# A gated convolution in sixteen array parts, plain v loaded in pieces, and a new fixed order

## The chip, the cores and the metric

The kernel runs on one core of a Trainium2 chip. The metric is the device time of one execution in microseconds (us). A core has five engines that run side by side, each with its own instruction stream: TensorE (PE; its weight loads are listed as PEld), VectorE (DVE), ScalarE (ACT), GpSimd (POOL) and SyncE (SP), which here only issues DMA transfers.

## The reference

Two layers stand one behind the other. The first is attention over 8 batches, 8 heads, 576 positions and 64 columns a head. Heads 0 to 3 look back over a plain window of 32 positions, heads 4 to 7 over every fourth of the last 128.

```python
scores = scale * np.matmul(q, k.transpose(0, 1, 3, 2))
mask_plain = (rel >= 0) & (rel < window)                                    # window 32
mask_dil = (rel >= 0) & (rel < window * dilation) & (rel % dilation == 0)   # dilation 4
attn = np.exp(scores - max); attn = attn / (attn.sum(-1) + 1e-9)            # masked scores are -1e9
x = np.matmul(attn, v)            # then heads side by side: (8, 576, 512)
```

The second is a gated linear unit with a causal convolution of five taps, each of the 512 channels for itself:

```python
for k in range(5):
    gate_pre += conv_w[k][None, None, :] * xp[:, k:k + S, :]                # xp: x with 4 zeros ahead
out = (1 / (1 + np.exp(-gate_pre)) * (x @ w_val)) @ w_out
```

Inputs and outputs are float32; the kernel computes in bfloat16 with float32 accumulation.

## The kernel before, in words

All work is cut into 733 tasks, each the instructions of one engine for one step. `plan.add(name, engines, function, deps, tens)` makes a task, and `ORDER` at the top of the file writes out in which order they are emitted and on which engine: `177P` is task 177 on TensorE, the letters being P, A, V, G, S for PE, ACT, DVE, POOL, SP, and a number behind the letter is a count of warm-up matmuls (L659) ahead of it. `HOMES` says which buffer of its class (`COUNTS`) each tensor takes. Every engine works through its own part of that order from first to last, so a task that waits holds up all tasks of its engine that stand behind it.

Per batch there is a plain half and a dilated half, and each consists of two units of two heads:

- SP loads q, k and v. Plain v (`load_vp`, tile `vp`) comes in runs of 64 floats: 18 runs a partition for the first four batches (`NAT`), 24 for the others, as one DMA. Dilated v (`vd`) is one DMA of longer runs. Loads marked `big` form a chain: each waits until the fifth big one before it has landed (`DEPTH`).
- POOL or ACT casts dilated v to bfloat16 (`vn`, task U), and for the first four batches moves rows of plain v to other partitions (`vw`, tasks HA to HD, `SHIFTS`).
- PE transposes q and k (L464 dilated, L401 plain), ACT or DVE copies them out (`qT`, `kT`).
- PE computes scores of three query blocks (L333, task S, 6 matmuls), ACT takes the exponential (L340), DVE multiplies with a mask (L347). PE multiplies with v (L356, task A, 12 matmuls; v has a column of ones for the sum), DVE takes the reciprocal (L365) and scales (L366, task N).
- PE transposes the result (L428 plain, 6; L488 dilated, 16), and a copy puts it into `xT`, channels on partitions.

Two batches form a group. `gated` cuts the 1152 positions of a group into three blocks of 384 columns, the last group into four of 288. For each block and each half `cp` of the channels (two chunks of 128) there are four tasks. The convolution (C) multiplies `xT`, shifted by the tap, with a diagonal matrix of weights, `conv_diag`, in 64x64 array parts: 5 taps x 2 chunks x 2 row halves are 20 matmuls (L530), and the four that stand together use the four different quarters of the array. ACT takes tanh (L540, task G; sigmoid is 0.5 + 0.5 tanh of half the argument), PE computes the values (L548, task V, 8 matmuls), and DVE multiplies (L558, task Y). One row half of every second chunk lands in the other half of the partitions; the rows and columns of w_val and w_out are permuted to fit when POOL casts them (tasks Wv and Wo), in 24 and 7 copies. Every value task waits for all of w_val, every output task for all of w_out.

`outputs` makes 36 tiles of 128 positions: 4 matmuls (L577, task O), an eviction on ACT (L584) or DVE (L586), a store by SP (L590).

PSUM, where PE writes, is cut into three two-bank buffers (`pd`, class `ps2`: scores, attention times v, plain transposes, convolution, values) and two one-bank buffers (`pu`, class `ps1`: dilated transposes, outputs). A convolution half takes one `pd`, its value task another.

Of the kernel before, what the change touches and what calls it, by code (L numbers as in the profile page):

```python
# [16 lines left out]
0G 15S 16S 1S 13S 33P6 14S 34A 48S 17S 47S 49S 2P 31P1 32A 3V 18G 38P2 57P 51G 21P 59V 22V 53G 58V 52G 39A 40V  # L17
19P 35P 20A 26P2 36A 23P 80S 27A 37V 24A 28V 25V 41P2 54P 56A 4S 55A 42V 29P 30V 70P 81S 6G 45P3 5G 43P 50A
60P 73P 7S 46V 71A 44A 74A 8G 112S 61A 96P 84P 63P 64A 149P 72V 97A 75V 76P 98P 85V 65V 62V 82S 66P 77V 86P
67V 150A 99A 100P 78P 87A 101A 83G 103P 88P 89A 79V 68P 69V 104A 113S 105V 119P 114S 120A 91P 92A 145P 151P  # L20
93V 102V 90V 121A 94P 169S 146A 152V 106P 95V 147P 122P 107V 108P 170S 110P 123V 124A 138P 109A 201S 139A 148V
135P 185P 136A 125P 128P 129A 126A 111V 165P 166A 140V 130V 137V 116G 127V 186V 234S 202S 157P 158A 187P 115G
118G 117G 141P 171S 175P 176A 188V 192P 193A 131P 142V 132V 173P 172G 174A 189P 190A 208P 209V 210A 143P 133P
177P 178A 180P 203S 134V 211P 235S 250P 144V 159P 181A 213A 212A 227P 228A 153P 154A 11S 238P 205G 251V 194V
179V 191V 160V 182V 239A 206A 195P 229V 196V 207A 167P 168V 204G 12G 183P 184V 155P 252P 224P 225A 214P 240P
215A 9S 253V 156V 199P 254P 241V 255A 226V 217P 218A 161P 230P 197P 162A 200A 324S 267S 236S 216V 219V 245P
256V 220P 198A 246A 231V 10G 625P 628P 221V 323S 266S 325S 237G 626A 257P 242P 243A 276P 629A 222P 326G 223A
258A 278A 277V 163P 341P 232P 303P 247V 244V 259V 233V 342V 304A 299P 300A 164V 339P 260P 248P 329P 305P 330A
340V 268S 261V 631P 630S 355S 384S 533S 627S 346P 356S 249V 343P 264P 306V 265V 273P 632A 347A 344A 348V 274V
275A 272A 345V 262P 301P 302V 279P 280A 292P 634P 635V 263A 349P 350V 327P 293A 328A 289P 281V 282P 283A 290A  # L30
284V 271G 270G 269G 643P 644A 637P 285P 291V 294V 400P 401V 286V 638A 334P 331P 335A 332A 336V 640P 641A 295P
388P 389A 358P 296V 360A 311P 312A 361P 363A 333V 359V 287P 362V 288V 297P 337P 298A 338V 385S 417S 374P 375A
319P 386S 320A 307P 308A 353P 351P 639S 377P 364P 354V 376V 313P 357S 469S 642S 416S 352A 378A 379V 365A 402P
321P 390P 314V 403V 407P 367P 322V 649P 366V 368A 391A 380P 309P 485P 408A 650A 381V 369V 310V 404P 392P 393A
405A 486V 646P 370P 647A 422P 419P 394V 371V 424V 423A 421A 645S 470S 651S 633S 502S 418S 655P 382P 438P 409V
395P 420A 439A 387G 396A 315P 316A 449P 656A 383V 406V 410P 652P 411V 450A 435P 531S 425P 372P 653A 436A 426A
440V 397V 373V 317P 658P 654S 530S 532S 471S 451P 487P 501S 318V 427V 437V 659A 473P 441P 488A 452V 398P 475P
442V 445P 399V 476A 447P 446A 474A 492P 493A 428P 661P 429A 448V 494V 430V 548P 549V 472G 489P 480P 507P 662A
490A 491V 536P 537V 481A 508A 443P 444V 660S 663S 565S 657S 564S 509A 431P 432V 482V 550P 551A 477P 478A 412P
504P 555P 413A 556A 479V 433P 434V 505A 506A 495P 496V 414P 453P 454A 415V 552P 483P 484V 553A 538P 664P 539A  # L40
523P 510P 511A 524A 520P 521A 676P 570P 665V 497P 567P 677A 569A 568A 554V 557V 571A 636S 461P 462A 522V 525V
572A 534S 667P 463P 503S 498A 666S 648S 455P 535G 670P 671A 526P 464V 668V 456V 527V 566S 673P 558P 682P 559V
674A 672S 669S 678S 583P 586P 587A 584A 499P 588V 683V 500V 457P 458A 465P 466A 513P 585V 459P 460V 528P 589P
529A 514A 590V 679P 680A 691P 573P 540P 541A 576P 574A 577A 685P 515V 512V 692V 686A 516P 681S 684S 687S 517V
467P 591P 518P 605P 468V 519A 597P 606A 601P 578V 575V 592V 543P 602A 688P 579P 542V 544A 598A 580V 599P 689A
545V 603P 581P 582A 600V 546P 694P 547V 604V 695A 697P 698V 609P 593P 560P 562P 561V 563A 610A 594A 595P 675S
696S 690S 699S 703P 700P 704V 596V 701V 607P 608V 706P 709P 611P 612V 705S 702S 693S 621P 617P 710V 613P 622A
711S 707A 708S 715P 712P 716A 618A 713A 614A 615P 616V 714S 619P 623P 721P 722A 718P 719A 620V 624V 727P 717S
723S 720S 724P 728A 725A 729S 726S 730P 731A 732S
"""  # L50

HOMES = "01010210000113130211000021002000132000231120022230241102145110103141020101013010110671123222114010302002121011010121100020122020000113021121100010231011014002232122312230001402035111113121011000001040001271122022114211200220201210102211110120022006000113012301031011031312015002120122131011400020471110130403021302202101000612230101122001201213021121220010101202202400001311141011120300130017102102012110131140321053111213132000031220020210061030221022401013242000210112021202210011202120011203140201100102021003120310041312140112140011020113140211031200110403"
# [11 lines left out]
 'gate': 3,  # L64
# [38 lines left out]
class Plan:  # L103
# [28 lines left out]
    def run(self):  # L132
# [24 lines left out]
def kernel(  # L157
# [28 lines left out]
    GW = 384  # L186
    DA = D + 1
# [31 lines left out]
    ident2 = consts.tile([128, D], BF16, name="ident2")  # L219
# [3 lines left out]
    conv_diag = consts.tile([128, NCH, K, D], BF16, name="conv_diag")  # L223
# [6 lines left out]
    def early():  # L230
# [26 lines left out]
        nc.vector.tensor_copy(ident2[0:64, :], ident[0:64, 0:64])  # L257
        nc.vector.tensor_copy(ident2[64:128, :], ident[64:128, 64:128])
# [35 lines left out]
    def load_vp(b, ten):  # L294
        nat = b < NAT

        def issue():
            if nat:
                o, a = vp[ten.idx][:, 0:18, 0:D], [[D, 128], [128 * D, 18], [1, D]]
            else:  # L300
                o, a = vp[ten.idx][:, :, 0:D], [[D, 128], [QB * D, 4 * NB], [1, D]]
            return nc.sync.dma_start(out=o, in_=src_ap(v, (b * H * S - (0 if nat else W)) * D, a))
        return [load(f"Lvp{b}", ten, issue)]

    SHIFTS = (("HA", ((1, 0, 64, 64, 0), (1, 64, 64, 0, 1)), 1.0),
# [196 lines left out]
    def gated(g, xb, w_ready):  # L502
# [3 lines left out]
        for k in range(n_blk):  # L506
# [13 lines left out]

            for cp in range(2):
                pc, gt, pv = Ten("ps2"), Ten("gate"), Ten("ps2")

                def conv(eng, cp=cp, pc=pc, c0=c0, mov=mov, dst=dst, wd=wd):
                    for kk in range(K):
                        for n in range(2):
                            for hb in range(2):
                                ob = hb if n == 0 else 1 - hb
                                rb = slice(64 * hb, 64 * hb + 64)
                                nc.tensor.matmul(  # L530
                                    out=dst(ps2[pc.idx][64 * ob:64 * ob + 64, n, 0:wd]),
                                    lhsT=conv_diag[rb, 2 * cp + n, kk, :],
                                    rhs=mov(2 * cp + n, rb, c0 + kk - (K - 1)),
                                    start=(kk == 0), stop=(kk == K - 1))
                t_c = plan.add(f"C{g}{k}{cp}", (PE,), conv,
                               deps=[x_done[(b, 2 * cp + n)] for b in last for n in range(2)] + [w_ready["conv"]],
                               tens=[pc, gt, xb], out=pc)
# [58 lines left out]
    def weights():  # L596
# [14 lines left out]
        def conv_e(eng):  # L611
            for to, n, c, frm, ch in ((0, 64, 0, 0, 0), (64, 64, 0, 0, 1), (0, 64, 1, 64, 0), (64, 64, 1, 64, 1), (0, 128, 2, 0, 2)):
# [5 lines left out]
                in0=ident2[:, None, :].to_broadcast([128, NCH * K, D]),  # L618
# [90 lines left out]
```

## Time and profile before

| | us |
|---|---|
| median of 3 runs (lowest, highest) | 173.76 (173.53, 174.15) |
| the profiled execution | 173.37 |
| its span, from the first to the last instruction | 171.7 |
| busy: PE, PEld, DVE, ACT, POOL | 153.0, 102.2, 121.7, 108.4, 44.2 |
| convolution matmuls (L530), 520 | 23.1 busy |
| value matmuls (L548), 208 | 34.9 busy |
| output matmuls (L577), 127 recorded | 33.4 busy |

The profile is one execution. Its page gives busy time by engine, the span in 40 slices (a digit is the busy share in tenths), the DMA queues, the chain of waits that ended last, the costliest groups of instructions, and the DMA issues. Group rows read: line, engine, operation, written tile <- read tiles, shapes, count | busy us, mean ns of one | idle time ahead of them and what ended it. In a table by windows each engine has its busy us and, in brackets, its instructions; then come the granted PE clock, the DMA share and GB/s. SPq is SP issuing. Matmuls are pipelined, so their single durations overlap, and some records of them can be missing.

### The profile page before, as it was taken

Reading aid. Unit: us, or ns where it says so; the run is one execution under the profiler, and the core shown is the slowest. Engines: PE = TensorE matmul, PEld = TensorE weight load, DVE = VectorE, ACT = ScalarE, POOL = GpSimd, SP = SyncE. Lnnn points to the kernel's source line nnn. Section 1 sums busy time; section 2 is a strip of 40 time slices with the busy share of each in tenths; the row PEclk is TensorE's granted clock in tenths of the full one; section 3 lists DMA queues with packets and bytes.
Section 4 is the critical chain, followed back from the end, with each engine's and each line's share of the span. In section 5 each row is a group of like instructions: output and inputs, shape, how many; then the busy total and the mean of one; then the engine's idle time right before and its main releaser. Section 6 shows DMA issues by size and latency. Waiting matters only on the chain.

```text
span 171.7 us, 5752 instructions
## 1 busy us (share of the span) xinstructions
PE 153.0 (89%) x2441; PEld 102.2 (60%) x2460; DVE 121.7 (71%) x243; ACT 108.4 (63%) x182; POOL 44.2 (26%) x82
## 2 busy tenths in 40 slices
PE   6697967888989979899999799989999999999990
PEld 1355654677557546567766567576656577666640
DVE  6549778989899579779788658899368776664220
ACT  2147976198868744798847693888946675242542
POOL 7023998560659427403000000210110000000000
PEclk9999999999999999999999999999999999999999
DMA  4999999999799999999994948969979060333445
GB/s 137 325 355 290 375 370 210 311 374 319 200 383 364 362 269 281 373 353 222 282 328 139 267 115 286 373 165 390 270 202 303 2 244 4 116 119 138 186 165 199
DMA packets 49123, 43.63 MB, mean 254 GB/s; under 512 B 22981, under 2 KB 39365, under 8 KB 49098
## 3 DMA queue, kind: packets, MB, share of 16 engines
q1 hardware_dynamic: 49098, 43.27, 82.2%
q8 instruction: 19, 0.31, 0.7%
q14 instruction: 6, 0.05, 0.1%
HBM read 33.83 MB, written 9.44 MB: 252 GB/s over the span
## 4 chain that ended last, share of the span: by engine, by line
PE 58%; DMA 12%; DVE 11%; ACT 6%; SPq 5%; issue 3%; POOL 3%; ACTq 0%; DVEq 0%; POOLq 0%
PE pu L577 17%; PE pd L548 14%; PE pd L530 9%; DMA qk<-in_k_dram 5%; PE pd L356 5%; DVE et L347 4%; DMA wt<-in_moe_w_out_dram 4%; SPq L281 4%; PE pd L333 4%; DMA qk<-in_q_dram 3%; PE pu L464 3%; POOL w_out L316 3%; PE pd L401 2%; PE pu L488 2%; ACT et L340 2%
## 5 line engine op out<-in xcount | busy, mean ns | idle before, releaser
L340 ACT ACTIVATE et<-pd 128x576 bf16<-128x576 f32 x64 | 39.3, 657 | 10.4 <-PE pd L333 9.3
L347 DVE TENSOR_TENSOR et<-et,mask 128x576 bf16<-128x576 bf16 x64 | 33.9, 557 | 4.7 <-ACT et L340 4.5
L548 PE MATMUL pd<-xT,w_val 128*128 128x384 bf16 (+1 forms) x208 | 34.9, 313 | 0.7 <-DVE xn L366 0.4
L577 PE MATMUL pu<-w_out,yT 128*128 128x512 bf16 x127 | 33.4, 379 | 1.4 <-issue 0.6
L558 DVE SCALAR_TENSOR_TENSOR yT<-gate,pd 128x768 bf16<-128x768 bf16 (+1 forms) x26 | 23.0, 886 | 12.5 <-PE pd L548 8.5
L366 DVE TENSOR_TENSOR xn<-pd,rec 96x768 bf16<-96x768 f32 x32 | 30.5, 954 | 1.1
L316 POOL CAST vn<-vd 128x1536 bf16<-128x1536 f32 x8 | 12.3, 1540 | 70.3 <-DMA vd<-in_v_dram 70.3
L540 ACT ACTIVATE gate<-pd 128x768 bf16<-128x768 f32 (+1 forms) x26 | 19.9, 769 | 10.9 <-DVE yT L558 5.5
L548 PEld LDWEIGHTS <-w_val 128*128 128x128 bf16 x208 | 19.4, 97 | 11.6 <-issue 1.5
L530 PE MATMUL pd<-xT,conv_diag 64*64 64x384 bf16 (+1 forms) x520 | 23.1, 313 | 1.8 <-DVE xT L314 1.1
L584 ACT ACTIVATE osb<-pu 128x512 f32<-128x512 f32 x27 | 16.2, 601 | 11.0 <-PE pu L577 10.7
L577 PEld LDWEIGHTS <-yT 128*128 128x128 bf16 x144 | 12.6, 97 | 13.3 <-issue 1.1
L333 PE MATMUL pd<-qT,kT 64*128 64x96 bf16 x384 | 16.1, 209 | 3.1 <-ACT qT L312 0.9
L530 PEld LDWEIGHTS <-conv_diag 64*64 64x64 bf16 x520 | 15.1, 106 | 6.2 <-issue 2.5
L316 POOL CAST vw<-vp 32x384 bf16<-32x384 f32 (+2 forms) x31 | 16.8, 541 | 7.5 <-DMA vp<-in_v_dram 6.1
L356 PEld LDWEIGHTS <-et 128*128 128x128 bf16 x384 | 14.7, 97 | 6.5 <-DVE et L347 2.5
L464 PE MATMUL pu<-ident,qk 128*128 128x128 bf16 x160 | 14.8, 230 | 3.0 <-DMA qk<-in_k_dram 2.0
L333 PEld LDWEIGHTS <-kT 64*128 64x128 bf16 x384 | 10.1, 96 | 11.5 <-issue 6.3
L464 PEld LDWEIGHTS <-qk 128*128 128x128 bf16 x160 | 10.8, 102 | 7.3 <-DMA qk<-in_k_dram 3.0
L314 DVE COPY xT<-pu 128x576 bf16<-128x576 bf16 x18 | 10.1, 568 | 4.0 <-PE pu L488 3.1
L312 ACT COPY xT<-pu 128x576 bf16<-128x576 bf16 x14 | 8.9, 646 | 6.2 <-PE pu L428 3.6
L365 DVE RECIPROCAL rec<-pd 96x12 f32<-96x12 f32 x32 | 7.1, 223 | 7.6 <-PE pd L356 4.5
(52 smaller groups left out, 146.2 us busy)
## 6 DMA issues: line engine op xcount, KB each, us to landing
out_dram<-osb SPq DMA_DIRECT2D x36, 256.0 KB, 2.7
vd<-in_v_dram SPq DMA_DIRECT2D x8, 768.0 KB, 9.3
qk<-in_k_dram SPq DMA_DIRECT2D x8, 576.0 KB, 7.8
qk<-in_q_dram SPq DMA_DIRECT2D x8, 576.0 KB, 8.0
qk<-in_q_dram SPq DMA_DIRECT2D x6, 640.0 KB, 9.1
qk<-in_k_dram SPq DMA_DIRECT2D x6, 640.0 KB, 8.7
vp<-in_v_dram SPq DMA_DIRECT2D x4, 768.0 KB, 7.9
vp<-in_v_dram SPq DMA_DIRECT2D x4, 576.0 KB, 9.8
```

What stands on the lines that cost most here:

```text
L316: nc.gpsimd.tensor_copy(out_, in_)
L333: nc.tensor.matmul(out=ps2[ps.idx][:, l, QB * jj:QB * jj + QB], lhsT=kT[kt.idx][rb, c:c + 128], rhs=qT[qt.idx][rb, c:c + QB], start=True, ...
L340: nc.scalar.activation(out=et[e.idx][:, 0:2 * HW].rearrange("p (l n) -> p l n", l=2), in_=ps2[ps.idx][:, :, 0:HW], func=AF.Exp, scale=scale)
L347: (nc.vector if eng == DVE else nc.gpsimd).tensor_tensor(out=ev, in0=ev, in1=m, op=ALU.mult)
L356: nc.tensor.matmul(out=ps2[po.idx][:, hf, (2 * jj + l) * DA:(2 * jj + l + 1) * DA], lhsT=et[es[hf].idx][:, c:c + 128], rhs=val(j, l), star ...
L366: nc.vector.tensor_tensor(out=xn[xt.idx][0:QB].rearrange("p (h j) l d -> p h (j l) d", h=2), in0=a[:, :, :, 0:D], in1=rr[:, :, :, None].to ...
L464: nc.tensor.transpose(out=o[:, f:f + 128], in_=a[:, c * RD + 128 * cb:c * RD + 128 * cb + 128], identity=ident)
L530: nc.tensor.matmul(out=dst(ps2[pc.idx][64 * ob:64 * ob + 64, n, 0:wd]), lhsT=conv_diag[rb, 2 * cp + n, kk, :], rhs=mov(2 * cp + n, rb, c0 ...
L540: nc.scalar.activation(out=gate[gt.idx][:, :, 0:wd], in_=ps2[pc.idx][:, :, 0:wd], func=AF.Tanh, scale=0.5)
L548: nc.tensor.matmul(out=dst(ps2[pv.idx][:, n, 0:wd]), lhsT=w_val[:, mc, c * 128:(c + 1) * 128], rhs=mov(mc, slice(0, 128), c0), start=(mc = ...
L558: nc.vector.scalar_tensor_tensor(out=yT[yb.idx][:, 2 * cp:2 * cp + 2, t0:t0 + wd], in0=gate[gt.idx][:, :, 0:wd], scalar=1.0, in1=ps2[pv.id ...
L577: nc.tensor.matmul(out=ps1[po.idx], lhsT=yT[yb.idx][:, c, c0:c0 + 128], rhs=w_out[:, c, :], start=(c == 0), stop=(c == NCH - 1))
```

## The change

The convolution of a block becomes one task for all four chunks, in 32x32 array parts: 5 taps x 4 chunks x 4 row groups are 80 matmuls, and the sixteen that stand together use sixteen different parts. It writes two `pd` buffers at once; ACT's tanh and the values follow in two halves as before. Now 32-row groups land permuted, so w_val and w_out are cast in finer pieces: 54 copies and 12. Plain v comes in pieces of 6 runs a partition (768 packets), three or four a batch, which are not part of the chain of big loads. There is a fourth `gate` buffer. `ORDER` and `HOMES` are new throughout: 743 tasks, with other places for loads, casts, evictions and output tasks, and a different share of copies between ACT and DVE; the first two dilated v casts and one group of shifts of batch 0 (HB) go to ACT, another (HA) comes from there. The third number of each `SHIFTS` entry changes too; the kernel does not use it.

```diff
- 'gate': 3,
+ 'gate': 4,
...
-            if t.load:
+            if t.load and eng == SP:
...
+    G = 32
...
-    ident2 = consts.tile([128, D], BF16, name="ident2")
+    ident2 = consts.tile([128, G], BF16, name="ident2")
...
-    conv_diag = consts.tile([128, NCH, K, D], BF16, name="conv_diag")
+    conv_diag = consts.tile([128, NCH, K, G], BF16, name="conv_diag")
...
-        def issue():
-            if nat:
-                o, a = vp[ten.idx][:, 0:18, 0:D], [[D, 128], [128 * D, 18], [1, D]]
-            else:
-                o, a = vp[ten.idx][:, :, 0:D], [[D, 128], [QB * D, 4 * NB], [1, D]]
-            return nc.sync.dma_start(out=o, in_=src_ap(v, (b * H * S - (0 if nat else W)) * D, a))
-        return [load(f"Lvp{b}", ten, issue)]
+        def issue(c):
+            o = vp[ten.idx][:, c:c + 6, 0:D]
+            step = 128 if nat else QB
+            return nc.sync.dma_start(out=o, in_=src_ap(v, (b * H * S - (0 if nat else W) + c * step) * D,
+                                                       [[D, 128], [step * D, 6], [1, D]]))
+        parts = [lambda c=c: issue(c) for c in range(0, 18 if nat else 4 * NB, 6)]
+        return [load(f"Lvp{b}", ten, part, big=False) for part in parts]
...
+            pcs, gts = [Ten("ps2") for _ in range(2)], [Ten("gate") for _ in range(2)]
+
+            def conv(eng, pcs=pcs, c0=c0, mov=mov, dst=dst, wd=wd):
+                for kk in range(K):
+                    for n in range(NCH):
+                        for r in range(4):
+                            ob = r ^ n
+                            rb = slice(G * r, G * r + G)
+                            nc.tensor.matmul(
+                                out=dst(ps2[pcs[n // 2].idx][G * ob:G * ob + G, n % 2, 0:wd]),
+                                lhsT=conv_diag[rb, n, kk, :], rhs=mov(n, rb, c0 + kk - (K - 1)),
+                                start=(kk == 0), stop=(kk == K - 1), tile_position=(G * r, G * ob))
...
             for cp in range(2):
-                pc, gt, pv = Ten("ps2"), Ten("gate"), Ten("ps2")
-
-                def conv(eng, cp=cp, pc=pc, c0=c0, mov=mov, dst=dst, wd=wd):
-                    for kk in range(K):
-                        for n in range(2):
-                            for hb in range(2):
-                                ob = hb if n == 0 else 1 - hb
...
+                pc, gt, pv = pcs[cp], gts[cp], Ten("ps2")
...
-                    for to, n, c, frm, ch in part:
-                        for h, st, g, sg in ((0, 3, 0, 1), (1, 1, 2, 1), (4, 3, 4, 2), (5, 1, 5, 2)):
-                            copy(eng, pair(w_val[to:to + n, 2 * pr + c, :], h, st), pair(i[frm:frm + n, ch, :], g, sg))
+                    to, n, c, frm, ch = part
+                    for a, b, w, m in ((0, 0, 64, 2), (128, 96, 32, 2), (160, 64, 32, 2), (256, 320, 64, 1), (320, 256, 64, 1),
+                                       (384, 480, 32, 1), (416, 448, 32, 1), (448, 416, 32, 1), (480, 384, 32, 1)):
+                        copy(eng, cols(w_val[to:to + n, 2 * pr + c, :], a, w, m, 64), cols(i[frm:frm + n, ch, :], b, w, m, 128))
```

More of the change, by code (lines that the diff above doesn't have):

```diff
@@ L22 @@
[L22 to L26, printed above, removed]
@@ new lines @@
+692P 693V 465P 592V 470P 471A 466V 606V 475P 474A 553V 557P 558V 695P 476V 468P 472P 469V 607P 611A 701P 473V
+696V 697S 682S 608A 694S 673S 593P 612P 594V 702A 703S 613V 573P 571P 574A 614P 618A 572A 615A 707P 708V 609P
+610V 709S 616P 617V 595P 698P 619P 596V 621P 689P 622A 625A 699V 704P 626P 690V 620V 700S 628P 627V 705V 722P
+725P 629A 726A 623P 691S 706S 723V 727S 724S 624V 710P 719P 720A 630P 711V 712S 721S 631V 728P 729A 632A 713P
+730S 714V 715S 633P 731P 732A 634V 734P 716P 733S 735A 736S 740P 717A 718S 737P 741A 742S 738A 739S
@@ L630, in wload, with cols @@
             return t, load(f"L{name}{pr}", t, issue)
-        def pair(a, h, step):
-            return a.rearrange("p (h d) -> p h d", d=D)[:, h:h + step + 1:step, :]
+        def cols(a, to, n, m, step):
+            return a[:, to:to + n] if m == 1 else a.rearrange("p (h d) -> p h d", d=step)[:, to // step:to // step + m, to % step:to % step + n]
         tw["val"], tw["out"] = [], []
-        for pr, parts in enumerate(((((0, 64, 0, 0, 0), (64, 64, 1, 64, 1)), ((64, 64, 0, 0, 1), (0, 64, 1, 64, 0))),
-                                    (((0, 128, 0, 0, 0), (0, 128, 1, 0, 1)),))):
+        for pr, parts in enumerate((((0, 64, 0, 0, 0), (64, 64, 1, 64, 1), (64, 64, 0, 0, 1), (0, 64, 1, 64, 0)),
+                                    ((0, 128, 0, 0, 0), (0, 128, 1, 0, 1)))):
             t, lw = wload("wv", moe_w_val, pr)
```

83 lines of the change are left out of this document (38 added, 45 removed), and 9 rows, old and new, of tables (SHIFTS, i).

## The prediction

> **What bounds the kernel now.** I read the page first: the busy shares and the 40 slices.
>
> ```profile
> PE 153.0 (89%) x2441; PEld 102.2 (60%) x2460; DVE 121.7 (71%) x243; ACT 108.4 (63%) x182; POOL 44.2 (26%) x82
> PE   6697967888989979899999799989999999999990
> DMA  4999999999799999999994948969979060333445
> HBM read 33.83 MB, written 9.44 MB: 252 GB/s over the span
> ```
>
> TensorE (PE) is nearly full in the last two thirds. The DMA engines are full in the first half and have holes behind that. So two regimes follow one another; the chain of waits shows where they meet.
>
> ```profile
> 50.82 0.62 POOL w_out L316
> ...
> 55.57 0.75 POOL w_out L316
> 56.36 0.38 PE pu L577
> ...
> 168.05 0.60 ACT osb L584
> ```
>
> The first output matmul (L577, task O0) starts at 56.36, right behind the seventh cast of w_out on GpSimd (POOL). From there the chain is nearly all PE, up to the last eviction at 168.05. I cut the span at these two times and asked for the busy time of each stretch.
>
> ```profile
> core 0: us, PE busy (x) PEld busy (x) DVE busy (x) ACT busy (x) POOL busy (x), PEclk, DMA share, GB/s
> 0.00:56.36 56.36, 46.45 (x787) 31.31 (x790) 44.98 (x108) 36.17 (x61) 32.43 (x69) 1.00 0.99 309
> 56.36:168.05 111.69, 106.52 (x1654) 70.90 (x1670) 76.76 (x136) 71.62 (x122) 11.75 (x13) 1.00 0.76 229
> 168.05:171.66 3.61, 0.00 (x0) 0.00 (x0) 0.00 (x0) 0.59 (x1) 0.00 (x0) 0.90 0.49 190
> ```
>
> Stretch A (56.36 us) waits for loads and for what POOL makes of them: DMA 0.99, PE slack in between. Stretch B (111.69 us) is PE: 106.52 busy, while DVE has 76.76, that is 69%. Stretch C (3.61 us) is the last store. The span 171.7 belongs to an execution of 173.37, so 1.7 us lie around it; the median of the runs, 173.76, is 0.4 above that. I work with the span and add both. About 0.3% (0.5 us) is what a measurement here can tell from no change.
>
> **The convolution.** Durations come from the chain, where each piece is a step on the path, and from the group of the convolution.
>
> ```profile
> L530 PE MATMUL pd<-xT,conv_diag 64*64 64x384 bf16 (+1 forms) x520 | 23.1, 313 | 1.8 <-DVE xT L314 1.1 <-DVE kT L314 0.3 <-ACT et L340 0.2
> 103.19 0.86 PE pu L577 x4
> 104.05 1.30 PE pd L548 x8
> ...
> 115.14 0.23 PE pd L333 x6
> ...
> 115.74 0.38 PE pd L356 x12
> 116.11 0.46 PE pu L488 x16
> ...
> 118.23 0.28 PE pu L464 x5
> ...
> 121.46 0.34 PE pu L488 x16
> ...
> 122.30 0.94 PE pd L530 x20
> ...
> 134.38 0.26 PE pu L428 x6
> ...
> 148.27 1.35 PE pd L530 x40
> ...
> 153.24 0.98 PE pd L548 x8
> ```
>
> 520 matmuls of 313 ns are 163 us of work in 23.1 us of time: the four 64x64 parts do run side by side. 23.1/130 rounds of four = 178 ns a round, and one full-array matmul of the same 384 columns takes 1.30/8 = 162 ns. So a round costs one stream plus a little, whatever the number of parts. The change makes rounds of sixteen: 1040 matmuls, 65 rounds. If a round still costs one stream, a whole block (80 matmuls) takes what half a block took: 0.94 us at 384 columns, 1.35/2 = 0.68 at 288. That halves 23.1 us, about 11.5 us saved, nearly all of it PE path.
>
> No row shows sixteen parts. From below: a round cannot be shorter than the stream, 5 x 162 ns = 0.81 us a block. From above: the closest pairs of weight load and matmul in the trace are the xn transposes, 16 in 0.34 us, 21 ns a pair. Sixteen parts need 0.94/80 = 12 ns a pair. If 21 ns were a floor, a block would take 1.7 us. I take 0.94, because those transposes are explained by their own streams and the fourfold rounds are the nearer row.
>
> The Trainium skill, TensorE: Matmul & The Clock Gate, Part 1 (Seeing it yourself), says that starts never come closer than about 25 ns however few the columns; by that a block would take an estimated 2.0 us and save nothing. The 21 ns above are already under it. The same page, Part 3, gives 10.6x for sixteen parts in one burst; by that, as an estimate, a round costs 1.5 streams and a block 1.2 us.
>
> **When stretch B begins.** POOL sets it again: output matmuls wait for both w_out tasks, and PE runs in a written order, so all behind the first output matmul waits too. The change cuts the permuted casts finer: w_val 54 copies for 24, w_out 12 for 7. Ahead of the w_out casts it leaves POOL 17 casts of shifted plain v (vw) and all of w_val, and moves the first two vn casts and three vw casts to ScalarE (two vw casts come back).
>
> ```profile
> 15.98 4.68 POOL L316 CAST vw<-vp 32x320 bf16<-32x320 f32 x8 [2.53 <-DMA vp<-in_v_dram]
> 20.72 6.92 POOL L316 CAST w_val<-wt 64x128 bf16<-64x128 f32 x24
> 31.60 5.87 POOL L316 CAST vw<-vp 32x320 bf16<-32x320 f32 x10 [2.32 <-DMA vp<-in_v_dram]
> L316 POOL CAST w_out<-wt 64x512 bf16<-64x512 f32 x6 | 4.6, 764 | 0.3
> L316 POOL CAST w_val<-wt 64x128 bf16<-64x128 f32 x16 | 4.5, 323 | 0.2
> ```
>
> Start: the vw casts began at 15.98 when the first plain v had landed; now 0.2 MB more is queued ahead of it, at 0.31 MB/us 0.7 us: 16.7. Then 17 vw casts at 5.87/10 = 0.59: 10.0. w_val: from 764 ns at 512 elements and 323 at 128, 1.15 ns an element; 6.92/24 = 0.29 a cast leaves 0.14 fixed; the elements stay, 30 casts are added: 6.92 + 30 x 0.14 = 11.1. w_out: 12 x 0.76 = 9.2 (32 partitions taken to cost as 64). Sum 47.0 instead of 56.4. Bounds: with w_val and w_out at their old totals, 16.7+10.0+6.9+5.5 = 39, where I set 43 because the transfers of w_out and PE's own work come in; with 0.29 for each of 54 small casts, 51.5.
>
> **What stretch B holds.** Counting PE's order behind the first output matmul: it now holds 3 value tasks (1.30), 4 attention-times-v (0.38), 5 score tasks (0.23), 4 transposes of dilated q/k (0.28), 2 of dilated xn (0.46) and 1 of plain xn (0.26) more: 3.9+1.5+1.2+1.1+0.9+0.3 = 8.9 us. Convolution there was 12 x 0.94 + 8 x 0.68 = 16.7 us, and is 8 x 0.94 + 4 x 0.68 = 10.2: 6.5 less (the rest of the 11.5 lay in A or moves out of it). B = 111.7 + 8.9 - 6.5 = 114.1 us, with the same idle 5 us as now.
>
> **What is late next: DVE.** Behind the first output matmul DVE too gets more.
>
> ```profile
> L347 DVE TENSOR_TENSOR et<-et,mask 128x576 bf16<-128x576 bf16 x64 | 33.9, 557 | 4.7 <-ACT et L340 4.5
> L366 DVE TENSOR_TENSOR xn<-pd,rec 96x768 bf16<-96x768 f32 x32 | 30.5, 954 | 1.1
> L365 DVE RECIPROCAL rec<-pd 96x12 f32<-96x12 f32 x32 | 7.1, 223 | 7.6 <-PE pd L356 4.5
> L558 DVE SCALAR_TENSOR_TENSOR yT<-gate,pd 128x768 bf16<-128x768 bf16 (+1 forms) x26 | 23.0, 886 | 12.5 <-PE pd L548 8.5
> L586 DVE TENSOR_SCALAR osb<-pu 128x512 f32<-128x512 f32 x9 | 6.2, 685 | 2.2 <-PE pu L577 2.2
> 100.00:120.00 20.00, 19.24 (x341) 13.18 (x341) 17.32 (x31) 15.31 (x27) 1.68 (x1) 1.00 0.83 272
> ```
>
> 6 masks (0.53 each), 3 norms (1.18), 3 gate products (0.89), 7 more output evictions (0.69; ScalarE gets 7 fewer): 3.2+3.5+2.7+4.8 = 14.2 us, 91 in all. Behind the last norm of the order stand 8 products, 7 evictions and a copy, 11 us; so 80 us of DVE lie in the part of B up to that norm. PE has 24 us behind it (15 output tasks 12.9, 8 value tasks 7.8, 3 blocks 2.0, transposes 1.2), so that part is 90 us long: DVE at 89%. The 20 us shown have 17.32, 87%. I let DVE run at 87%: 92 us, and add 2 us, 3 with handoffs between two nearly full engines. Cover gone (DVE at 80% there) would be 10 more.
>
> **Plain v in pieces.** 24 more DMA issues on SP, same packets and bytes.
>
> ```profile
> 22.43 0.37 SPq L302 DMA_DIRECT2D vp<-in_v_dram  x1
> 23.82 5.13 SPq L281 DMA_DIRECT2D qk<-in_q_dram  x1
> 28.00:31.00 3.00, 1.96 (x31) 1.31 (x30) 2.96 (x5) 0.71 (x1) 1.28 (x1) 1.00 0.67 129
> 126.12 0.39 SPq L302 DMA_DIRECT2D vp<-in_v_dram  x1
> ```
>
> Behind a plain v load SP hangs 5.13 us in its next issue, and the DMA engines then run dry (0.67, 129 GB/s). Other issues take some 0.4 us. Pieces should let loads be queued between them; 24 x 0.4 = 10 us of SP time lie beside everything. The gain is no term of its own: A is set by POOL, B by PE and DVE. It is the condition for B: the last plain v must be there when its attention comes. Behind that place PE's order holds 38 us of tasks (19 output tasks, 13 value tasks, 6 blocks and small ones, at the durations above), so it comes at about 164 - 38 = 126. Before, that load was issued at 126.12 and landed some 5 us later, the time that SP hangs behind one. The load side needs 37 MB (33.83 and the 12 stores ordered ahead, 0.26 each); at the 309 GB/s of stretch A that is 120 us. It fits by 6 us.
>
> Edits with one answer: conv_diag half as wide, four small identity copies on DVE, a fourth gate buffer, warm-up matmuls: all lie in A beside POOL; nothing.
>
> **Sum.** 47.0 + 114.1 + 3 = 164.1; + 3.6 (C) = 167.7 span; + 1.7 = 169.4; the median stands 0.4 higher, 169.8. I say 169.5.
>
> **Rivals.** (1) Less is late than I think: POOL done at 43, DVE adds nothing: 169.5 - 4 - 3 = 162.5. For it: both terms are bounds. (2) Pair floor: sixteen parts are fed at 21 ns a pair, 1.7 us a block. In B up to the last norm PE then has 8 x 0.74 = 6 us more against DVE's lead of 3, in the tail 3 x 1.0 more: +6, 175.5; by 25 ns a pair, 179. It turns slower from about 1.5 us a block. For it: nothing under 21 ns is sustained in the trace. Against: a round of four costs one stream. (3) Pieces do not help: the queue holds the same packets, SP hangs as before, the last plain v lands at 131 as before, 5 us late: 174.5. For it: three or four pieces of one batch often stand in a row. (4) Two-bank accumulators: a block now holds two of three pd buffers until two tanh are done, so scores, norms and values queue for the third and DVE stays at 80%: 10 instead of 3, 176.5. (5) The terms cancel to within 0.3%: 174.
>
> **Numbers.** Forecast (165 to 173) 0.47, rival 1 0.24, rival 2 0.10, rival 3 0.07, rival 4 0.07, rival 5 0.05. Faster 0.71, same 0.05, slower 0.24. Range 162 to 177: from rival 1 to rivals 2 to 4; the forecast's own is 165 to 173.
>
> **What would show it.** Conv group: 1040 matmuls, busy near 12 us; 1.7 us pieces in the chain mean rival 2. POOL: w_out casts end at 47 (43 to 51) and the first L577 stands right behind. Stretch B near 117 with DVE about 87% until the last norm. SP: no issue over 2 us behind a vp piece and no load-phase hole; last vp landed before 126. The forecast is wrong if B is PE idle for over 10 us, or if the first output matmul is not behind POOL.

## The result, and the profile after

The changed kernel takes 179.37 us (median of 4 runs, 177.04 to 180.68) against 173.94 for the kernel before on the same chip: 1.0272 times as long, 95% interval 1.0213 to 1.0330. I had predicted 169.5, with 162 to 177 as the range. It is slower, and outside the range.

The page of the profile after (an execution of 179.63): span, busy time, PE's 40 slices and its granted clock.

```profile
span 177.9 us, 6891 instructions
...
PE 151.6 (85%) x2972; PEld 101.4 (57%) x2996; DVE 121.0 (68%) x249; ACT 107.0 (60%) x174; POOL 53.3 (30%) x121
...
PE   6486668888759999886999959989999999999991
...
PEclk9999999999978999999999999999999999999999
```

PE's row has holes that the row of before lacks, a 7 and a 5 in slices 11 and 12, a 6 in slice 19 and a 5 in slice 24. The clock row has a dip at the first of them. GpSimd has 9 us more work than before (53.3 for 44.2).

GpSimd's timeline up to the output matmuls, then PE's around the first of them:

```profile
17.15 2.21 POOL L317 CAST vw<-vp 64x384 bf16<-64x384 f32 x4 [12.81 <-DMA vp<-in_v_dram]
19.42 4.64 POOL L317 CAST w_val<-wt 64x128 bf16<-64x128 f32 x18
24.12 1.61 POOL L317 CAST vw<-vp 32x384 bf16<-32x384 f32 x3
27.00 6.76 POOL L317 CAST w_val<-wt 128x128 bf16<-128x128 f32 x27 [1.27 <-DMA wt<-in_moe_w_val_dram]
33.83 6.19 POOL L317 CAST vw<-vp 32x320 bf16<-32x320 f32 x10
40.08 1.85 POOL L317 CAST w_val<-wt 128x128 bf16<-128x128 f32 x9
41.99 8.79 POOL L317 CAST w_out<-wt 64x512 bf16<-64x512 f32 x12
...
50.84 0.58 PE L579 MATMUL pu<-w_out,yT 128*128 128x512 bf16 x1 [2.02 <-POOL w_out L317]
```

The casts of w_out end at 50.78, and PE stood still 2.02 us for them. So stretch A is 50.84 us (56.36 before, 47.0 forecast). Stretch B, up to the end of the last output matmul at 174.40, and four windows (the first begins 3.8 us ahead of B):

```profile
50.84:174.40 123.56, 115.63 (x2371) 78.52 (x2390) 89.48 (x159) 75.42 (x126) 19.50 (x26) 0.99 0.69 218
...
47.00:60.00 13.00, 9.70 (x174) 6.18 (x170) 8.24 (x14) 6.15 (x10) 11.61 (x17) 0.87 1.10 336
60.00:80.00 20.00, 18.17 (x447) 13.33 (x451) 16.80 (x30) 14.31 (x24) 6.88 (x12) 1.00 0.78 254
80.00:100.00 20.00, 17.77 (x304) 12.25 (x303) 15.82 (x32) 14.89 (x27) 1.47 (x1) 1.00 0.99 274
100.00:120.00 20.00, 17.38 (x456) 13.09 (x454) 16.48 (x34) 15.78 (x28) 1.61 (x1) 1.00 0.97 316
```

B is 123.6 us instead of 117. Between 80 and 120 PE has 17.8 and 17.4 busy of 20, and DVE only 15.8 and 16.5: neither is full. The chain of waits tells what PE does there (start, us, what):

```profile
55.13 1.10 PE pd L530 x80
...
77.81 1.16 PE pd L530 x80
...
82.86 1.75 issue
...
103.76 1.80 issue
...
146.88 0.98 PE pd L530 x80
```

The convolution's group beside it:

```profile
L530 PE MATMUL pd<-xT,conv_diag 32*32 32x384 bf16 (+1 forms) x1040 | 14.7, 314 | 0.6 <-DVE xn L367 0.5
```

A block of the convolution takes 1.10 to 1.16 us, 0.98 at 288 columns. And there are two steps named "issue", 1.75 and 1.80 us, in which PE waited for no semaphore. (A third in the chain, 1.37 at 58.88, is DVE's.) The longest step of that name in the chain of before:

```profile
31.03 0.84 issue
```

PE's waits from 50 to 178 us, longest first (total, times, longest), say the same:

```profile
PE pu L579 <- POOL w_out L317: 2.0, 1, 2.0
PE pd L334 <- issue: 1.8, 1, 1.8
PE pd L357 <- issue: 1.8, 1, 1.8
```

PE's timeline shows the first of the two:

```profile
80.93 1.90 PE L579 MATMUL pu<-w_out,yT 128*128 128x512 bf16 x7
82.67 0.19 PE L357 MATMUL pd<-vw,et 128*128 128x65 bf16 x1
84.61 0.20 PE L357 MATMUL pd<-vw,et 128*128 128x65 bf16 x1 [1.75 <-issue]
```

PE stops in the middle of twelve matmuls of one task. What the DMA queue of instructions moved from 81.7 to 83.0:

```profile
q8 instruction: 1, 0.02, 5.2%
```

It is one packet of 16 KB, at 81.8; from 72.3 to 81.7 this queue had none. Since the packet before it (71.2) PE had executed 496 weight loads and matmuls, where in before it has some 250 between two on the mean. The second pause stands behind a packet at 103.1, after 446.

The loads did what I had said, in part: where pieces of plain v stand in a row, each still holds SP for 1.2 to 2.0 us on the mean,

```profile
108.71 6.02 SPq L301 DMA_DIRECT2D vp<-in_v_dram  x3
...
116.86 4.91 SPq L301 DMA_DIRECT2D vp<-in_v_dram  x4
```

but the last is issued by 121.8, before 126, and PE waits for no plain v in B.

Some executions were disturbed and took longer: the differences below are between medians of the others (after: 179.1, three of four; e1: 174.27, one of four), and the profiles of e1, e9, e10 and e11 are of disturbed ones, so that only single steps are read from them.

### The profile page after: what moved, and what is told of

Its sections match the earlier page's. It is cut to its first block, busy times and chain, and to the rows that moved or that the text cites. A ratio compares the mean times of both kernels' runs of the same rounds, so it can differ in the third digit from the quotient of the medians.

```text
span 177.9 us, 6891 instructions
## 1 busy us (share of the span) xinstructions
PE 151.6 (85%) x2972; PEld 101.4 (57%) x2996; DVE 121.0 (68%) x249; ACT 107.0 (60%) x174; POOL 53.3 (30%) x121
## 4 chain that ended last, share of the span: by engine, by line
PE 52%; POOL 12%; SPq 9%; DVE 8%; issue 7%; DMA 6%; ACT 4%; POOLq 0%; ACTq 0%; DVEq 0%
PE pu L579 15%; PE pd L550 14%; PE pd L530 7%; DMA wt<-in_moe_w_val_dram 6%; POOL w_val L317 5%; POOL w_out L317 4%; PE pd L357 4%; SPq L301 3%; PE pd L334 3%; POOL vw L317 3%; PE pd L402 3%; PE pu L465 2%; DVE xn L367 2%; PE pu L429 2%; SPq L282 2%
## 5 line engine op out<-in xcount | busy, mean ns | idle before, releaser
L579 PE MATMUL pu<-w_out,yT 128*128 128x512 bf16 x124 | 34.6, 385 | 3.6 <-POOL w_out L317 2.0
L348 DVE TENSOR_TENSOR et<-et,mask 128x576 bf16<-128x576 bf16 x64 | 31.3, 515 | 2.8 <-ACT et L341 2.7
L317 POOL CAST vw<-vp 32x384 bf16<-32x384 f32 (+2 forms) x37 | 19.8, 536 | 18.2 <-DMA vp<-in_v_dram 16.3
L317 POOL CAST vn<-vd 128x1536 bf16<-128x1536 f32 x6 | 9.0, 1493 | 47.9 <-DMA vd<-in_v_dram 45.0
L334 PE MATMUL pd<-qT,kT 64*128 64x96 bf16 x384 | 17.8, 210 | 5.7 <-issue 1.8
L586 ACT ACTIVATE osb<-pu 128x512 f32<-128x512 f32 x20 | 12.0, 599 | 15.6 <-PE pu L579 15.2
L334 PEld LDWEIGHTS <-kT 64*128 64x128 bf16 x384 | 10.9, 96 | 13.1 <-issue 6.4
L588 DVE TENSOR_SCALAR osb<-pu 128x512 f32<-128x512 f32 x16 | 11.0, 689 | 8.8 <-PE pu L579 8.0
L530 PE MATMUL pd<-xT,conv_diag 32*32 32x384 bf16 (+1 forms) x1040 | 14.7, 314 | 0.6 <-DVE xn L367 0.5
L317 POOL CAST w_val<-wt 64x64 bf16<-64x64 f32 (+5 forms) x54 | 13.1, 291 | 1.5 <-DMA wt<-in_moe_w_val_dram 1.3
L530 PEld LDWEIGHTS <-conv_diag 32*32 32x32 bf16 x1040 | 10.7, 88 | 4.0 <-issue 2.0
```

Of the source, the lines that this page charges most:

```text
L317: nc.gpsimd.tensor_copy(out_, in_)
L334: nc.tensor.matmul(out=ps2[ps.idx][:, l, QB * jj:QB * jj + QB], lhsT=kT[kt.idx][rb, c:c + 128], rhs=qT[qt.idx][rb, c:c + QB], start=True, ...
L348: (nc.vector if eng == DVE else nc.gpsimd).tensor_tensor(out=ev, in0=ev, in1=m, op=ALU.mult)
L530: nc.tensor.matmul(out=dst(ps2[pcs[n // 2].idx][G * ob:G * ob + G, n % 2, 0:wd]), lhsT=conv_diag[rb, n, kk, :], rhs=mov(n, rb, c0 + kk - ( ...
L579: nc.tensor.matmul(out=ps1[po.idx], lhsT=yT[yb.idx][:, c, c0:c0 + 128], rhs=w_out[:, c, :], start=(c == 0), stop=(c == NCH - 1))
```

## The experiments

My theory after the comparison: three things ate the gain. GpSimd's casts are longer than I summed; the sixteen-part blocks take 1.10 instead of 0.94; and 520 more pairs of weight load and matmul make PE outrun its instructions. The rival: the new order costs the time, whatever the convolution does.

**e1: the old casts.** After, with w_val and w_out cast in 24 and 7 copies as before (the channels then stand in mixed order).

```diff
-for a, b, w, m in ((0, 0, 64, 2), (128, 96, 32, 2), ...): copy(eng, cols(...), cols(...))
+for h, st, g, sg in ((0, 3, 0, 1), (1, 1, 2, 1), (4, 3, 4, 2), (5, 1, 5, 2)): copy(eng, pair(...), pair(...))
```

> The changed kernel with the casts of w_val and w_out cut as before (24 and 7 copies); everything else as changed. The 32-row groups then meet weights in the old permutation, so output channels are mixed; the amount of work is that of the reference. Theory (the price of sixteen parts lies on POOL): in the changed kernel the first output matmul comes at 50.84, right behind 13.3 us of w_val casts and 8.8 us of w_out casts; with 6.9 and 5.5 the last cast ends 9.7 us sooner, near 41 to 43, the granted clock stays full (it fell to half for 3.4 us at about 50), and the time is 170 to 172. Rival (the two-bank accumulators or the new order itself hold stretch B): the first output matmul comes as early, but B grows by most of what A loses; time 176 or more.

174.27, 4.8 less than after; but the median of all four executions is 177.4 (up to 177.75), only 2.0 less than that of after. So the gain lies somewhere between 2 and 5 us, and is not known closer. The end of GpSimd's casts and the first output matmuls in the timeline:

```profile
41.90 2.58 POOL L317 CAST w_out<-wt 64x512 bf16<-64x512 f32 x4 [1.69 <-DMA wt<-in_moe_w_out_dram]
...
48.61 1.04 PE L579 MATMUL pu<-w_out,yT 128*128 128x512 bf16 x3
```

The casts end at 44.5, the first output matmul stands at 48.6 all the same: 2.2 us under the casts lies another bound, the order of PE and DVE (its rows stand at e2, which has the same casts). In B the first of the two pauses remains, in the chain (a step of 1.31 at 83.57 there is output matmuls at half clock):

```profile
79.87 1.71 issue
```

**e2: four parts.** e1 with the convolution in four 64x64 parts, a whole block in one task.

```diff
-    G = 32
+    G = 64
...
-                        for r in range(4):
-                            ob = r ^ n
+                        for r in range(2):
+                            ob = r ^ (n % 2)
```

> The changed kernel with the old casts and with the convolution of a block in four 64x64 parts (40 matmuls a block, still one task on two pd buffers, so that order and buffers are those of the changed kernel). Theory: against the sixteen parts with the same casts, PE has 8 blocks of 1.9 instead of 1.10 us and 4 of 1.36 instead of 0.98 behind the first output matmul, 7.9 us more, less about 3.6 us if the two pauses of 1.75 and 1.80 us without a semaphore (82.9 and 103.8 in the changed kernel) go with the 1040 extra PE instructions: 174 to 178. Rival (order and accumulators decide, DVE is the bound): within 2 us of the sixteen parts with the same casts.

177.99 (177.82 to 178.17), ratio to before 1.0246, interval 1.0211 to 1.0281. Two blocks of its chain:

```profile
51.22 1.76 PE pd L530 x40
...
143.93 1.35 PE pd L530 x40
```

What PE does just ahead of the first output matmul, in its timeline:

```profile
47.95 0.30 PE L334 MATMUL pd<-qT,kT 64*128 64x96 bf16 x6 [1.50 <-DVE yT L560]
48.19 1.04 PE L579 MATMUL pu<-w_out,yT 128*128 128x512 bf16 x3
```

PE waits 1.50 us for a gate product of DVE, and the output matmul follows at 48.2: with the short casts A hangs on that.

No "issue" step over 0.84. So order, pieces and buffers alone cost 4.5 us against before: the first output matmul comes 8.2 us sooner (48.2 for 56.4), and from there to the end of the last one it takes 13.1 us longer (124.8 for 111.7). Sixteen parts bring 0.6 to 3.7 (e1) or lose 1.1 (after), though a block is shorter by 0.66 and 0.37 us. Order and task sizes of e2 and after agree, so I paired the 1,956 weight loads outside the convolution one by one and noted where their difference in start jumps. Behind the start of the output matmuls:

| | us |
|---|---|
| 8 blocks of 384 columns, 0.66 each; 4 of 288, 0.37 each | -6.8 |
| wait for w_out (48.4 against 50.8) | +2.2 |
| stretch at half clock, 50.9 to 54.3 | +1.5 |
| pause at 82.9 | +1.9 |
| pause at 103.8 | +2.0 |
| the rest, with 0.2 from stretch A | +0.6 |
| sum; the spans are 176.5 and 177.9 | +1.4 |

So in this pair of executions the saving of the sixteen parts is there, and is spent.

**e3: a warm clock.** After, with eight warm-up matmuls ahead of an early output task, against the half clock.

```diff
-641P 150P
+641P8 150P
```

> The changed kernel with eight warm-up matmuls ahead of the first output matmul, where PE stands idle from 47.1 to 50.8 and the granted clock falls to half for 3.4 us. Theory (half clock costs what PE does in that time at half speed, 1.7 us): the clock stays at 1.00, time 177.5. Rival (PE is not the bound there, or the pause of the clock has another cause): unchanged, 179.

180.93 (179.55 to 181.61): no gain. In the profile the half clock at 50.9 is gone, but another stands at 26.2 to 29.6; it lies ahead of the warm-ups (49.2), so it is not their doing, and e4 and e13 have one there too. The first pause is longer:

```profile
79.35 3.28 issue
```

So a price of the half clock alone is not shown by a run; the 1.5 above is one pair of traces.

**e4: plain v whole.** After, with each plain v in one DMA at the place of its second piece.

```diff
         def issue(c):
-            o = vp[ten.idx][:, c:c + 6, 0:D]
+            if c != 6:
+                return None
+            o = vp[ten.idx][:, 0:runs, 0:D]
```

> The changed kernel with plain v again in one DMA a batch, issued where its second piece stood. Theory (the load side is ahead of PE in the changed kernel; pieces neither gain nor cost): 179 within 1.5 us. Rival 1 (pieces help): SP hangs 5 us behind each, holes in the transfers, 182 or more. Rival 2 (24 more issues hurt): 177 or less.

181.78 (181.08 to 183.5), 2.7 slower than after. In this order the pieces help. Through what is not separated: the profile has three stretches at half clock where after has one, and two pauses again, one of them in another place:

```profile
103.32 1.47 issue
...
124.25 2.42 issue
```

**e5: more instructions in the kernel before.** Each convolution matmul in two halves of its columns.

```diff
+for hv in range(2):
     for kk in range(K): ...
-        out=dst(...), rhs=mov(...)
+        out=cut(dst(...)), rhs=cut(mov(...))
```

> The kernel before, with each convolution matmul cut in two halves of its columns: 1,040 instead of 520, the same products and the same number of streamed columns. Theory (TensorE's instruction stream: the profile after shows two pauses of 1.75 and 1.80 us with no semaphore, each behind a late fetch of 16 KB of instructions, and the kernel before none): the profile shows at least one such pause of 1.5 to 3 us between 60 and 130 us, and the time is 175.5 to 179. Rival A (the pauses belong to the thirty-two-row parts, not to the number of instructions): no such pause, conv busy up from 22 to 24-28 us for the doubled number of weight loads, time 174 to 175.5. Rival B (the pauses belong to the order of after): no pause, and the time of before, 173.5 to 174.3.

175.21 (174.58 to 177.19) against 173.56; ratio 1.012, interval 1.0034 to 1.0206. The chain has one step above 0.81 us without a semaphore, at 40.4, behind an instruction packet at 39.0:

```profile
40.38 1.09 issue
```

The longest hole between 60 and 130, in PE's timeline, has a semaphore:

```profile
87.67 1.46 PE L550 MATMUL pd<-xT,w_val 128*128 128x384 bf16 x8 [1.77 <-ACT et L340]
```

Instructions cost time here too, 1.7 us, but a pause without a semaphore between 60 and 130, as my theory has it, is not there. Two facts of the trace leave it open: the hole begins 0.6 us behind an instruction packet (85.3) that came after 473 weight loads and matmuls, as the pauses of after do, and it ends 0.35 us after the exponential that the profile names. Rival A has the time right and the convolution wrong (23.5 us busy, 23.1 before, not 24 to 28). The run does not decide.

**e6: pieces in the kernel before**, back to back at the place of the one DMA.

```diff
+for c in range(0, 18 if nat else 4 * NB, 6):
     r = nc.sync.dma_start(out=vp[ten.idx][:, c:c + 6, 0:D], in_=...)
```

> The kernel before, with each load of plain v issued in pieces of 768 packets one behind the other at the place of the one transfer. Theory (pieces let go of SP earlier but the queue hangs in them for 1.7 to 2 us each all the same, so that back to back they are worth nothing; what they gained in after came from their separate places): 173.5 to 174.3, and the pieces together occupy the queue for 4.5 to 6 us. Rival (smaller transfers interleave better with the others that are under way and the waits of 1 to 2 us behind plain v in the kernel before go): 171.5 to 173.

173.76 against 173.56, ratio 1.0022 (0.9995 to 1.0049): nothing. Three pieces in a row hold SP for 7.1 to 8.0 us here, more than I expected. That pieces gain something in after because other loads stand between them fits e4 and this run, but no run changes that alone.

**e7: rows by DMA in after.** The loads of w_val and w_out put rows in their place, so GpSimd casts 128 partitions at once; HC0 moves ahead.

```diff
-5G 7G 57G 85S
+57G 5G 7G  85S
...
-return nc.sync.dma_start(out=wt[t.idx]..., in_=src_ap(w, pr * 256 * Dm, ...))
+for to, n, c, nc_, frm, step in rows:
+    r = nc.sync.dma_start(out=wt[t.idx]...[to:to + n, c:c + nc_, :], in_=src_ap(w, (pr * 256 + frm) * Dm, ...))
```

> The kernel after, with the rows of w_val and w_out put in their place by the transfers that load them (eleven more DMA issues), so that GpSimd casts 128 partitions at a time: 36 instructions for w_val instead of 54, 4 for w_out instead of 12; and the head casts that HC0 makes stand ahead of the first w_val casts in GpSimd's order. Theory (GpSimd's row of casts sets the first output matmul, 50.8 us in after; w_out's casts shrink from 8.8 to 3-4 us and w_val's from 13 to 9-11): the casts of w_out end at 41 to 45 us, the first output matmul stands at 43 to 47, and the time is 173.5 to 176. Rival (with that row shorter the start is bound by TensorE's and VectorE's own order, near 48 us, as with the coarse casts): first output matmul at 47.5 to 49.5, time 176.5 to 178. Second rival (the eleven issues on SP delay the loads behind them): q and k heads late by 1 to 3 us, time 178 to 181.

180.99 (179.72 to 181.8), 1.9 slower than after. GpSimd's last cast of w_out and PE's first output matmuls in the timeline, then the chain:

```profile
45.08 0.62 POOL L317 CAST w_out<-wt 128x512 bf16<-128x512 f32 x1 [0.26 <-DMA wt<-in_moe_w_out_dram]
...
48.38 1.04 PE L579 MATMUL pu<-w_out,yT 128*128 128x512 bf16 x4
```

```profile
46.37 9.90 DMA qk<-in_k_dram
...
83.31 1.62 issue
```

The casts end at 45.7 as the theory said, the output matmuls start at 48.4 as its rival said, and then a load of k that takes 9.9 us holds PE until 56.3: the second rival. A does not hang on GpSimd alone; the order of PE and DVE stands right below, and so do the loads.

**e9: the same in the kernel before**, nothing else; w_out is cast in 4 copies instead of 7.

```diff
-for to, n, c, frm, ch in parts:
-    copy(eng, w_out[to:to + n, 2 * pr + c, :], i[frm:frm + n, ch, :])
+for c in range(2):
+    copy(eng, w_out[:, 2 * pr + c, :], i[:, c, :])
```

> The kernel before, with nothing else changed than that the rows of w_val and w_out are put in their place by the transfers that load them: GpSimd casts w_out in 4 instructions of 128 partitions instead of 7. Theory (the casts of w_out are what the first output matmul waits for at 56.4 us in the kernel before, 5.5 us of casts behind the transfer): they take 2.5 to 3.5 us, the first output matmul stands at 53 to 54.5, and the time is 170.5 to 172. Rival (the transfers of w_out, now in five to seven issues, land later by as much, or the work before the output matmuls is late anyway): the first output matmul stands at 55.5 to 57 and the time is 173 to 174.5.

174.94 (173.7 to 177.03) against 173.56: ratio 1.0064, interval 1.0036 to 1.0092, slower by 0.6%. The expected 2 us did not come; where they went is open.

**e10 and e12: more instructions in four parts.** e2 with halved convolution matmuls: 1,040 pairs, the same streams. e12 is the same kernel again, for a profile at full clock.

```diff
+for hv in range(2):
     for kk in range(K): ...
-        out=dst(ps2[...]), rhs=mov(n, rb, c0 + kk - (K - 1))
+        out=cut(dst(ps2[...])), rhs=cut(mov(n, rb, c0 + kk - (K - 1)))
```

> The kernel with the convolution in four parts and the coarse casts in the order of after (178.0 us), with each convolution matmul cut in two halves of its columns: 1,040 instead of 520, the same products, the same streamed columns. Theory (a pause comes where TensorE's instructions run faster than they are fetched, whatever their parts): one or two pauses of 1.5 to 3 us without a semaphore, as in the kernel before with the same cut (one of 1.74, 175.2 against 173.6), and 179.5 to 181.5. Rival (pauses belong to thirty-two-row parts): none, and 177.5 to 179.

> The kernel in four parts with halved convolution matmuls once more, for a profile at full clock: the last one ran at a granted clock of 0.85 throughout, at which TensorE takes its instructions more slowly. Theory (the number of instructions makes the pauses): at full clock one to three pauses of 1 to 3 us without a semaphore between 50 and 130 us, 180 to 181.5 us. Rival (the second weight load of each half costs TensorE's time itself): no pause, but convolution blocks longer than the 1.8 us that they take at full columns, by 0.2 us each.

181.24 (e10) and 181.58 (e12, of 180.72 and 182.44), against 178.0 for e2: 3.2 to 3.6 us for 520 pairs that add no streamed column. (The pause of 1.74 in the kernel before that the text on e10 counts is the hole at 87.67 above, which has a semaphore.) The profile of e10 is of an execution of 191.46 us at a granted clock of 0.85, and its chain has no "issue" step over 0.84, against my theory. The chain of e12:

```profile
74.38 1.85 PE pd L532 x80
...
80.12 1.13 issue
...
146.36 1.38 PE pd L532 x80
```

Blocks are longer than in e2 by only 0.03 us (1.78 to 1.85, 1.38), so the pairs themselves cost next to nothing. Paired with e2 as above, 2.5 us stand between the last output matmuls, and 2.4 of them in two jumps: 1.3 at the pause shown, behind a packet that came after 490 instructions, and 1.1 at 105.9 to 106.8, in the middle of a transpose task and right behind another packet, where the profile names DVE. So a pause does not need thirty-two-row parts; the size is at the lower end of what I expected.

**e11: three taps of five**, in sixteen parts.

```diff
-for kk in range(K): ... stop=(kk == K - 1)
+for kk in range(3): ... stop=(kk == 2)
```

> The kernel after with only three of the convolution's five taps: it leaves out two fifths of the convolution, 624 matmuls instead of 1,040, in sixteen parts all the same. Theory (the number of instructions makes the pauses): no pause over 1.5 us without a semaphore after 55 us; a block of 48 pairs takes 0.65 to 0.75 instead of 1.10 and 0.98; thirteen blocks by 0.36 are 4.7, the two pauses 3.5: 170 to 172.5. Rival (the pauses belong to the order or to the sixteen parts): they stay, one or two of 1.5 to 2 us, and the time is 173.5 to 175.5. Second rival (VectorE and the hand-overs set the pace in this stretch, not TensorE): 177 to 180 whatever the convolution takes.

172.17 (170.81 to 174.51); 171.8 in the comparison, 7.3 less than after. Chain:

```profile
55.18 0.74 PE pd L530 x48
...
102.54 1.13 issue
...
146.72 0.66 PE pd L530 x48
```

A block loses 0.36 (0.32 at 288 columns): nine and four blocks are 4.5. Both pauses of after are gone, one of 1.13 us comes; the packet ahead of it came after 306 instructions. 4.5 + 3.55 - 1.13 = 6.9. The second rival (VectorE sets the pace) is out.

**e13: half of the columns**, 1,040 pairs kept.

```diff
-out=dst(...), rhs=mov(n, rb, c0 + kk - (K - 1))
+out=cut(dst(...)), rhs=cut(mov(n, rb, c0 + kk - (K - 1)))
```

> The kernel after with each convolution matmul run over half of its columns only (the other half of the convolution is left out): 1,040 pairs as in after, half of the streamed columns. Theory (a block of 80 pairs is bound by the feeding of weight loads and matmuls, 8.3 ns a pair after the first rounds): a block takes 0.75 to 0.95 instead of 1.10 and 0.98, not half; the pauses stay, one to three of 1.5 to 3 us; the time is 176 to 178.5. Rival (a block is bound by its streams, five rounds of 160 ns at 384 columns): 0.55 to 0.65 a block, 172 to 175.

177.25 (174.81 to 178.22); 176.1 in the comparison, only 3.0 less than after. Chain:

```profile
74.83 0.92 PE pd L531 x80
...
79.63 2.08 issue
...
142.74 0.81 PE pd L531 x80
```

Half of the streams takes 0.24 us off a block and leaves a pause of 2.08 (and one of 1.03 at 119.7). e11 with 416 pairs fewer won 7.3 us, e13 with the same pairs and fewer columns won 3.0: in this kernel the number of convolution instructions weighs more than their columns.

No version here that does the whole convolution is shown to beat the kernel before.

## Why the prediction was wrong

Span forecast 167.7, measured 177.9: A is 3.8 over, B 6.5, C 0.1 under. Four steps failed: the price of the w_val casts (3.4 us with the wait in them), the length of a sixteen-part block (2.7), and two costs that had no term, PE's pauses (3.6) and the half clock (at most 1.7).

**Stretch A (47.0, measured 50.84): the step that failed is w_val.** Start 17.15 (16.7 forecast), vw 2.21 + 1.61 + 6.19 = 10.0 (10.0), w_out 8.79 (9.2) were right. w_val took 4.64 + 6.76 + 1.85 = 13.25 instead of 11.1: 54 casts cost 0.245 each where my fixed 0.14 and the elements made 0.206. And I summed without a wait; one of 1.27 for the second w_val transfer came. Still within my bounds. e1, e2 and e7 (48.6, 48.2, 48.4) show that without it A would not have been under about 48.2 in this order: I named GpSimd as the only bound, and the 43 of rival 1 was out of reach.

**The convolution (0.94 and 0.68 a block, measured 1.10 to 1.16 and 0.98).** "A round costs one stream" holds: e11 takes two rounds off and 0.36 us, 0.18 a round, the 178 ns of the fourfold rounds. What I missed is that a block of five rounds has 0.20 on top (1.10 - 5 x 0.18), where ten rounds of four parts had none (1.76), and that at 288 columns a round costs 0.16, not 0.12. Over twelve blocks in B, 2.7 us. Of the two figures of the Trainium skill, TensorE: Matmul & The Clock Gate, that I set beside it, Part 3's 10.6x, worked out as an estimate of 1.2 us a block, was the closer. The floor of 25 ns from start to start in Part 1 (it stands there under Wait — 56ns, not 53.3ns?) is not seen: 80 pairs in 0.81 us (e13) are 10 ns a pair. Rival 2, 21 ns a pair and 1.7 us a block, is out for the same reason.

**Instructions (no term, measured 3.6).** No step of mine counted that 520 more pairs are 1,040 more instructions to bring to PE. The two pauses are 1.75 + 1.80. That their number is a cost is shown by e10 and e12 (+3.2 and +3.6 with nothing else changed) and by e11 against e13. That a late fetch is the mechanism is read from the traces and was not isolated. For it: packets come some 7 us apart, and of the twelve steps of 1 us or more in which PE waits for no semaphore, in the chains of all runs, eleven begin within 1.6 us behind the start of one (that of e3 begins 0.5 us ahead). Against a plain count: those packets came after 306 to 504 instructions (380 and 320 in e4), while packets after 398 to 416 in after, e1 and e2 brought no step of that length; and e5 gave no such pause where I expected one.

**Clock (no term, at most 1.7).** 3.41 us at half clock right behind the wait for w_out; before had a full clock up to its last output matmul.

**DVE (3, about 1.6 left).** 2.7 + 3.55 + 1.7 = 7.9 is 1.4 more than the 6.5 that B is over, so by subtraction some 1.6 of my 3 are left. From 60 to 120 DVE ran at 82%, not 87%, near the 80% of rival 4. But rival 4's cause, scores and norms queueing for the third buffer, would show as waits of PE, and from 50 to 178 PE's waits for DVE and ACT sum to 2.5 us, none over 0.4. So DVE was not late next, and PE, with its pauses, gave it less to do.

**Plain v in pieces (0, right in effect).** SP hangs in pieces as rival 3 said, but they end before 126 and bind nothing; e4 gives them 2.7 us in this order. There are 20 more issues, not 24 (28 of plain v for 8).

**Moved work (8.9) and rest: right in their sum.** The trace of after has just the tasks behind the first output matmul that I counted. With blocks of 1.76 and 1.35 for 0.94 and 0.68 my sum for four parts is 169.4 + 8 x 0.82 + 4 x 0.67 = 178.6; e2 has 178.0. Part of that is luck: the sum keeps the 47.0 for A, where e2 has 48.2, and the 3 for DVE, which longer blocks should shrink. So in this order the forecast of a gain rested on the sixteen parts, and there, and in the casts that go with them, the error lies.

The mark that I set myself for "wrong", PE idle over 10 us in B, is not met by the record (123.56 - 115.63 = 7.9): a slow clock and longer blocks count as busy. The other mark is not met either: the first output matmul does stand behind POOL.

## What to carry to other kernels

Packing the array multiplies the instructions while it divides the streams: price a packed form by its blocks and by its number of weight loads and matmuls, and look in the chain for steps that wait for no semaphore. When several engines and queues are nearly full at a handover, removing the one that the chain names uncovers the next within a few microseconds (48.2 to 48.6 under 50.8 here), so a bound is worth only the distance to the second one. And test a change in the order in which it will run: pieces of a load were worth 2.7 us spread in one order and nothing back to back in the other.

## What the runs showed of the hardware

- Sixteen 32x32 parts are fed at 10 to 14 ns a pair of weight load and matmul: a block of 80 pairs takes 1.10 us at 384 columns, 0.86 to 0.92 at 192, 0.81 at 144. If the 0.20 that a block has on top stays, a round cannot go under about 0.12 to 0.13 us, 8 ns a pair (an estimate from these).
- PE can stop for 1.0 to 3.3 us with no semaphore to wait for, in the middle of a task; in after, e1, e3, e4, e7, e12 and e13, with more than 2,970 matmuls in the record, at least one such step above 1.1 us lies between 79 and 125 us; in before, e2, e6 and e9, with under 2,480, none. e11 (2,580) has one of 1.13, and e5 (2,980) one of 1.09, at 40. e10 (2,996), at a granted clock of 0.85, has none.
- In after a wait of 2 us at 48.8 was followed by 3.41 us at half the granted clock (50.9 to 54.3). With eight warm-up matmuls there (e3) this stretch did not come, but one stood at 26.2, ahead of them, and the time did not fall.
